# Sliding-window attention into a SwiGLU block: gather offsets in another order, batch 1's value products one place later, two more second-softmax transposes on the DMA crossbar

## The chip, the cores and the metric

The kernel runs on one core of a Trainium2 chip. The metric is the device time of one execution in microseconds (us); the time before is the median of three runs. Five engines work side by side, each through its own list of instructions in order: TensorE (PE), VectorE (DVE), ScalarE (ACT), GpSimd (POOL) and SyncE (SP). POOL and SP also issue DMA transfers, each on a queue of its own (q0 is POOL's, q1 is SP's), and sixteen DMA engines serve both queues.

## The reference

Attention over 8 batches of 8 heads, 576 positions and 64 dimensions, and behind it a gated feed-forward block over the 8 x 576 = 4608 tokens of 512 channels:

```python
mask = np.abs(pos[:, None] - pos[None, :]) <= 32
mask = mask | is_global[:, None] | is_global[None, :]      # 8 global positions
scores = np.where(mask, q @ k.T / sqrt(64), -1e9)
x = softmax(scores) @ v                                     # (b, h, s, d) -> (b*s, h*d)
g = x @ w_gate                                              # 512 -> 1536
out = (g * sigmoid(g) * (x @ w_val)) @ w_out                # 1536 -> 512
```

## The kernel before, in words

The feed-forward block is the backbone. The 4608 tokens are cut into nine chunks of 512, and a chunk is sixteen units: twelve `gate` units (one 128-wide slice of the hidden layer: four matmuls `pg`, four matmuls `pv`, then a tanh `th` on ACT and the products `gv` and `h` on DVE) and four `outp` units (twelve matmuls `po` each, a copy `osb` on ACT and a store). Between two units there is a gap with a number, and the attention of the next batch is dealt out over these gaps by a table written by hand: each batch's function `attention(b)` returns a dictionary from gap to steps. Batch 1's numbers count from gap 3, batch 2's from gap 16, batch 3's from gap 32, and so on by 16. Nothing reorders the steps afterwards: what stands in a gap stands there on every engine.

The steps of a batch, with the names of their tiles:

- `step_GT` turns the gathered and masked rows of the global keys and queries (`kqm`) on PE and copies them on DVE to `gT`.
- `step_S2` multiplies all keys `kT` by the global queries (the second softmax: global rows against all columns). ACT makes `p2e`, DVE multiplies it by the mask to `p`. `step_SG` multiplies all queries `qT` by the global keys in the same way (`pge`, `pg`). `step_S2` needs `kT` and `gT`, `step_SG` needs `qT` and `gT`.
- `step_P2T` turns `p` around into `p2t`. Below the batch number `XP` five PE transposes and one ACT copy do it; from `XP` on, one DMA transpose on SP's queue.
- `step_AV2` multiplies `p2t` by the values `va`; DVE makes `gvt` of it.
- `step_S(0..4)` are the score products of the window; ACT makes `pe`, DVE masks it to `pt`. `step_AV(0..3)` and `step_AV8` multiply these by `va`, by a copy of the values moved by 64 partitions (`vb`), and by `gvt`; DVE normalises to `xa`. `step_AV(tp)` needs the buffer `m` in PSUM that the one before it leaves when it is normalised.
- `step_X(tp)` turns `xa` into the block's input `xT`, from batch 2 on by DMA transposes on SP's queue.

From batch 2 on, keys and queries are first cast to bf16 in DRAM by POOL's queue (`kf`, `qf`) and then turned by two DMA transposes on SP's queue (`kT`, `qT`). Batch 0 runs ahead of the backbone in a head section, in which PE fills its waits with dummy matmuls `ps_w`. The head begins with small tables: a chain of short DVE instructions makes the row numbers `gofs` from which POOL's indirect DMAs gather the global rows `kg` and `qg`. POOL's loads of `va` and the weights stand behind these gathers. `va_clear` sets the borders of `va` by four memsets.

Of the kernel before, what the change touches and what calls it, by code (L numbers as in the profile page):

```python
# [9 lines left out]
FP32 = mybir.dt.float32  # L10
BF16 = mybir.dt.bfloat16
I32 = mybir.dt.int32
I64 = mybir.dt.int64
AF = mybir.ActivationFunctionType
ALU = mybir.AluOpType
AX = mybir.AxisListType

P = 128


def bc(ap, dims):

    return bass.AP(tensor=ap.tensor, offset=ap.offset, ap=[ap.ap[0]] + dims)
# [3 lines left out]
def kernel(  # L27
# [34 lines left out]
    const = ctx.enter_context(tc.tile_pool(name="const", bufs=1))  # L62
# [70 lines left out]
    gidx_i64 = const.tile([P, NG], I64)  # L133
# [6 lines left out]
    def load_0(name, hg):  # L140
# [13 lines left out]
    bofs_f = const.tile([P, 2, B // 2], FP32)  # L154
    nc.gpsimd.iota(bofs_f, pattern=[[0, 2], [2 * H * S, B // 2]], base=0, channel_multiplier=0,
                   allow_small_or_imprecise_dtypes=True)
# [40 lines left out]
    dmh = const.tile([P, 2, 2], FP32)  # L197
    nc.vector.tensor_tensor(out=dmh, in0=dmask[:, 0:2], in1=dmask[:, 2:4], op=ALU.add)
    mka = const.tile([P, 2, 2], FP32)
    nc.vector.tensor_reduce(  # L200
        out=mka, in_=oh16.rearrange("p h a r -> p a r h"), axis=AX.X, op=ALU.add
    )
    asel = const.tile([P, 2], FP32)
    nc.vector.tensor_reduce(out=asel, in_=mka, axis=AX.X, op=ALU.add)
    va_clear(0)
    hb = const.tile([P, 2], FP32)
    nc.vector.tensor_scalar(
        out=hb, in0=bc(asel[:, 1:2], [[-1, 2]]), scalar1=float(H * S), scalar2=None, op0=ALU.mult
    )
    nc.vector.tensor_tensor(  # L210
        out=bofs_f, in0=bofs_f, in1=bc(hb, [[1, 2], [0, B // 2]]), op=ALU.add
    )
# [6 lines left out]
    gidx_f = const.tile([P, NG], FP32)  # L219
    nc.vector.tensor_copy(  # L220
        out=gidx_f, in_=gidx_i64.bitcast(I32).rearrange("p (a b) -> p a b", b=2)[:, :, 0]
    )
    tmp8 = const.tile([P, NG], FP32)
    gcol = const.tile([P, 1], FP32)
    nc.vector.tensor_tensor(out=tmp8, in0=p8, in1=gidx_f, op=ALU.mult)
    nc.vector.tensor_reduce(out=gcol, in_=tmp8, axis=AX.X, op=ALU.add)
    ngcol = const.tile([P, 1], FP32)
    nc.vector.tensor_scalar(out=ngcol, in0=gcol, scalar1=-1.0, scalar2=None, op0=ALU.mult)
    nc.vector.tensor_scalar(
        out=hrow, in0=hrow, scalar1=float(S), scalar2=gcol, op0=ALU.mult, op1=ALU.add  # L230
    )
    nc.vector.tensor_scalar(out=gofs, in0=bofs_f, scalar1=hrow, scalar2=None, op0=ALU.add)
    R2 = (WIN + 0.5) ** 2
    thr = const.tile([P, 2], FP32)
    nc.vector.tensor_scalar(
        out=thr, in0=asel, scalar1=R2 + 0.25, scalar2=-0.25, op0=ALU.mult, op1=ALU.add
# [3 lines left out]
        out=sgn, in0=asel, scalar1=2.0, scalar2=-1.0, op0=ALU.mult, op1=ALU.add  # L240
# [2 lines left out]
    nc.vector.tensor_scalar(  # L243
        out=thi, in0=asel[:, 0:1], scalar1=1e6, scalar2=0.5, op0=ALU.mult, op1=ALU.add
    )

    def gather(i):
        kg = gw.tile([P, D], FP32, tag="kg", name="kg")
        qg = gw.tile([P, D], FP32, tag="qg", name="qg")
        for a, (dst, src) in enumerate(((kg, k), (qg, q))):  # L250
            nc.gpsimd.indirect_dma_start(
                out=dst, out_offset=None,
                in_=src.rearrange("b h s d -> (b h s) d"),
                in_offset=bass.IndirectOffsetOnAxis(ap=gofs[:, a, i : i + 1], axis=0),
            )
        return kg, qg
# [91 lines left out]
    def attention(b):  # L348
# [354 lines left out]
        L = lambda f, *a: (lambda: f(*a))  # L703
# [30 lines left out]
        if b == 1:  # L734
            return r | {
                5: [L(step_P2T), L(step_S, 0)],
                6: [L(step_S, 1), L(step_AV2)],
                7: [L(step_S, 2), L(step_AV, 0)],
                8: [L(step_S, 3), L(step_AV, 1)],
                9: [L(step_AV, 2)],  # L740
                10: [L(step_AV, 3), L(step_X01, 0)],
                11: [L(step_S, 4), L(step_X01, 1)],
                12: [L(step_AV8)], 13: [L(step_X8)],
            }
# [162 lines left out]
    for i, g in attention(1).items():  # L907
        gaps[3 + i] = gaps.get(3 + i, []) + g
# [56 lines left out]
```

## Time and profile before

| | |
|---|---|
| median of 3 runs | 357.86 us (357.67 to 358.93) |
| the profiled execution | 357.59 us |
| its span, first to last instruction | 355.7 us |
| PE busy | 348.3 us, 98% |
| DVE, ACT, POOL busy | 231.6, 151.9, 93.7 us |
| granted TensorE clock | 0.999 |

The profiled execution took 1.9 us more than its span, and 0.27 us less than the median. PE is nearly always at work, so a time on another engine or a queue counts only where PE waits for it.

### The profile page before, as it was taken

To read this page: it belongs to the slowest core of one execution; us is meant where nothing else is said; L and a number is where in the kernel's file an instruction comes from. 1 tells how busy PE (TensorE), PEld (TensorE's weight loads), DVE (VectorE), ACT (ScalarE), POOL (GpSimd) and SP (SyncE) were. 2 spreads that over 40 slices of the span, in tenths; PEclk is the share of its full clock that TensorE was granted. 3 is DMA by queue.
4 is the path that set the end of the run, shared out by engine and by line. 5 is a ranking of instruction groups with operands and counts; after the bars stand their busy time and mean duration, and the time that the engine had idled before them with its cause. 6 is when DMAs were issued, how large, how long until landed. Compare 5 with 4: busy or idle time off the path is not lost.

```text
span 355.7 us, 7729 instructions
## 1 busy us (share of the span) xinstructions
PE 348.3 (98%) x3161; PEld 168.0 (47%) x3161; DVE 231.6 (65%) x470; ACT 151.9 (43%) x235; POOL 93.7 (26%) x110
## 2 busy tenths in 40 slices
PE   7999999999999999999999999999999999999996
PEld 2574545444444454444444444444444444444444
DVE  5868784389818873789368935894488637815850
ACT  4865662465325541554244523543254323323322
POOL 8894663905325214301290111000000000000000
PEclk9999999999999999999999999999999999999999
DMA  7999999999999999995899979813330230011002
GB/s 104 156 196 204 184 211 161 166 252 141 157 166 233 140 155 153 180 180 80 147 164 157 138 120 168 115 40 92 101 73 2 61 100 28 0 59 62 0 20 101
DMA packets 153541, 44.15 MB, mean 124 GB/s; under 512 B 140065, under 2 KB 148001, under 8 KB 153505
## 3 DMA queue, kind: packets, MB, share of 16 engines
q0 software_dynamic: 101216, 19.14, 67.2%
q1 hardware_dynamic: 52288, 24.51, 33.2%
q8 instruction: 25, 0.41, 0.5%
q14 instruction: 12, 0.09, 0.1%
HBM read 38.02 MB, written 16.52 MB: 153 GB/s over the span
## 4 chain that ended last, share of the span: by engine, by line
PE 84%; DMA 9%; POOL 4%; DVE 1%; issue 1%; SPq 0%; ACT 0%; POOLq 0%
PE po L850 26%; PE pg L793 24%; PE pv L793 23%; DMA va<-in_v_dram 5%; PE ps_av L595 3%; PE ps_s L508 3%; DMA q_bf<-in_q_dram 3%; DMA vb<-va 2%; PE ps_av L586 1%; PE po L837 1%; POOL va L102 1%; PE ps_av L477 1%; PE ps_s L442 1%; PE ps_av L622 0%; PE ps_av L614 0%
## 5 line engine op out<-in xcount | busy, mean ns | idle before, releaser
L793 PE MATMUL pg<-xT,wg_sb 128*128 128x512 bf16 x420 | 108.1, 380 | 0.0
L793 PE MATMUL pv<-xT,wv_sb 128*128 128x512 bf16 x420 | 107.8, 379 | 0.0
L822 DVE SCALAR_TENSOR_TENSOR gv<-th,pg 128x512 bf16<-128x512 bf16 x107 | 73.3, 685 | 50.5 <-ACT th L820 49.5
L820 ACT ACTIVATE th<-pg 128x512 bf16<-128x512 f32 x107 | 63.9, 598 | 81.7 <-PE pg L793 81.2
L850 PE MATMUL po<-wo_sb,h 128*128 128x512 bf16 x420 | 94.6, 380 | 0.0
L826 DVE TENSOR_TENSOR h<-gv,pv 128x512 bf16<-128x512 bf16 x107 | 73.5, 687 | 11.5 <-PE pg L793 0.5
L793 PEld LDWEIGHTS <-wv_sb 128*128 128x128 bf16 x424 | 41.5, 98 | 50.0
L850 PEld LDWEIGHTS <-h 128*128 128x128 bf16 x420 | 39.5, 98 | 45.4
L793 PEld LDWEIGHTS <-wg_sb 128*128 128x128 bf16 x424 | 38.4, 98 | 43.5 <-issue 1.7
L102 POOL DMA_DIRECT2D va<-in_v_dram x40 | 35.0, 982 | 82.5 <-PE ps_av L595 77.7
L855 ACT ACTIVATE osb<-po 128x512 f32<-128x512 f32 x35 | 20.9, 597 | 81.9 <-PE po L850 79.9
L541 ACT ACTIVATE pe<-ps_s 128x1024 bf16<-128x1024 f32 (+1 forms) x39 | 36.4, 936 | 17.1 <-PE ps_s L508 17.1
L547 DVE TENSOR_TENSOR pt<-pe,band 128x1024 bf16<-128x1024 bf16 (+1 forms) x39 | 24.7, 634 | 14.0 <-ACT pe L541 14.0
L568 DVE TENSOR_TENSOR xa<-ps_av,den 128x512 bf16<-128x512 f32 (+1 forms) x40 | 25.5, 638 | 1.4
L562 DVE TENSOR_REDUCE den<-ps_av 128x8 f32<-128x16 f32 (+1 forms) x40 | 6.7, 167 | 27.6 <-PE ps_av L595 25.2
L508 PEld LDWEIGHTS <-kT 64*128 64x128 bf16 x576 | 10.7, 95 | 15.5 <-issue 15.1
L109 POOL DMA_DIRECT2D kf<-in_k_dram x6 | 13.4, 2240 | 15.9 <-issue 9.3
L109 POOL DMA_DIRECT2D qf<-in_q_dram x6 | 16.0, 2667 | 1.5 <-DMA qf<-in_q_dram 1.5
L508 PE MATMUL ps_s<-qT,kT 64*128 64x64 bf16 x576 | 15.3, 191 | 0.0
L595 PE MATMUL ps_av<-vb,pt 128*64 128x66 bf16 x256 | 14.2, 197 | 0.8 <-DMA vb<-va 0.8
L595 PE MATMUL ps_av<-va,pt 128*64 128x66 bf16 x256 | 14.4, 197 | 0.0
L595 PEld LDWEIGHTS <-pt 128*64 128x64 bf16 x512 | 10.8, 110 | 5.0 <-DMA vb<-va 0.9
(142 smaller groups left out, 200.3 us busy)
## 6 DMA issues: line engine op xcount, KB each, us to landing
out_dram<-osb SPq DMA_DIRECT2D x35, 256.0 KB, 2.3
vb<-va SPq DMA_DIRECT2D x14, 264.0 KB, 6.0
kf<-in_k_dram POOLq DMA_DIRECT2D x6, 576.0 KB, 16.4
qf<-in_q_dram POOLq DMA_DIRECT2D x6, 576.0 KB, 18.5
va<-in_v_dram POOLq DMA_DIRECT2D x24, 128.0 KB, 11.3
va<-in_v_dram POOLq DMA_DIRECT2D x16, 96.0 KB, 7.8
wg_sb<-in_moe_w_gate_dram POOLq DMA_DIRECT2D x3, 512.0 KB, 11.5
wv_sb<-in_moe_w_val_dram POOLq DMA_DIRECT2D x3, 512.0 KB, 13.3
```

The lines of the kernel that those rows point to most:

```text
L102: nc.gpsimd.dma_start(out=va[lo:hi, u, :, 0:D], in_=vs[t0 + lo : t0 + hi])
L109: nc.gpsimd.dma_start(out=t, in_=src[b].rearrange("h s d -> s h d"))
L508: nc.tensor.matmul(out=ps[:, par, 64 * slot : 64 * slot + 64], lhsT=kT[r : r + 64, hp, 64 * t : 64 * t + P], rhs=qTs[b][r : r + 64, hp, 64 ...
L541: nc.scalar.activation(out=pe, in_=ps[:, :, 0 : 64 * ns].rearrange("p r (s c) -> p r s c", c=64), func=AF.Exp, scale=SCALE,)
L547: mult = lambda: nc.vector.tensor_tensor(out=pt.rearrange("p r s c -> p (r s) c"), in0=pe.rearrange("p r s c -> p (r s) c"), in1=bc(band, ...
L568: nc.vector.tensor_tensor(out=xa.rearrange("p (g h) d -> p g h d", g=g), in0=bc(ps, pst + [[1, D]]), in1=bc(den, [[4, g], [1, 4], [0, D]]) ...
L595: nc.tensor.matmul(out=ps[64 * e : 64 * e + 64, hg, hl, :], lhsT=pt[:, hl % 2, 4 * (hl // 2) + 2 * (tp % 2) + e, :], rhs=(va if e == 0 els ...
L793: nc.tensor.matmul(out=ps[:, 0:n], lhsT=w[:, cc, P * fc : P * (fc + 1)], rhs=xT[:, cc, t0 : t0 + n], start=(cc == 0), stop=(cc == NCC - 1),)
L820: nc.scalar.activation(out=th[:, 0:n], in_=pg[:, 0:n], func=AF.Tanh, scale=0.5)
L822: nc.vector.scalar_tensor_tensor(out=gv[:, 0:n], in0=th[:, 0:n], scalar=1.0, in1=pg[:, 0:n], op0=ALU.add, op1=ALU.mult,)
L826: nc.vector.tensor_tensor(out=st["h"][:, fc, 0:n], in0=gv[:, 0:n], in1=pv[:, 0:n], op=ALU.mult)
L850: nc.tensor.matmul(out=po, lhsT=st["h"][:, fc, P * ts : P * (ts + 1)], rhs=wo_sb[:, fc, :], start=(fc == 0), stop=(fc == NFC - 1),)
```

## The change

There are three parts. First, the chain to `gofs`: the four memsets of `va_clear(0)` and the small table `dmh` go behind it, the base of the row numbers is now worked out from the table `i8_f` in place of a POOL iota of its own, the integer column is multiplied without a copy to float ahead of it, and everything is prepared up to the global column `gcol`, which comes in last. Second, batch 1's `step_AV(0)` and `step_AV(1)` go one gap later each. Third, `XP` is 2 in place of 4, so that batches 2 and 3 turn `p` by a DMA transpose on SP's queue too; in batch 2 `step_S2`, `step_SG` and `step_P2T` go to its gap 2 (they stood in gaps 3, 3 and 4), and `step_S(2)`, `step_AV(0)`, `step_S(3)`, `step_AV(1)` and their `step_X` go one gap earlier; in batch 3 `step_P2T` goes from gap 4 to gap 2.

```diff
-    XP = 4
+    XP = 2
...
-    va_clear(0)
-    hb = const.tile([P, 2], FP32)
-    nc.vector.tensor_scalar(
-        out=hb, in0=bc(asel[:, 1:2], [[-1, 2]]), scalar1=float(H * S), scalar2=None, op0=ALU.mult
-    )
-    nc.vector.tensor_tensor(
-        out=bofs_f, in0=bofs_f, in1=bc(hb, [[1, 2], [0, B // 2]]), op=ALU.add
-    )
...
+    hb = const.tile([P, 2], FP32)
+    nc.vector.tensor_scalar(
+        out=hb, in0=bc(asel[:, 1:2], [[-1, 2]]), scalar1=float(H), scalar2=hrow,
+        op0=ALU.mult, op1=ALU.add,
     )
+    bofs_f = const.tile([P, 2, B // 2], FP32)
+    nc.vector.scalar_tensor_tensor(
+        out=bofs_f, in0=bc(i8_f, [[0, 2], [1, B // 2]]), scalar=float(2 * H),
+        in1=bc(hb, [[1, 2], [0, B // 2]]), op0=ALU.mult, op1=ALU.add,
+    )
+    nc.vector.tensor_scalar(out=bofs_f, in0=bofs_f, scalar1=float(S), scalar2=None, op0=ALU.mult)
...
+    nc.vector.tensor_scalar(out=gofs, in0=bofs_f, scalar1=gcol, scalar2=None, op0=ALU.add)
...
+    va_clear(0)
...
-                7: [L(step_S, 2), L(step_AV, 0)],
-                8: [L(step_S, 3), L(step_AV, 1)],
-                9: [L(step_AV, 2)],
+                7: [L(step_S, 2)],
+                8: [L(step_S, 3), L(step_AV, 0)],
+                9: [L(step_AV, 1), L(step_AV, 2)],
...
-                3: [L(step_S2), L(step_SG)],
-                4: [L(step_S, 0), L(step_P2T)],
+                2: [L(step_S2), L(step_SG), L(step_P2T)],
+                4: [L(step_S, 0)],
                 6: [L(step_S, 1), L(step_AV2)],
-                8: [L(step_S, 2), L(step_AV, 0), L(step_X, 0)],
-                10: [L(step_S, 3), L(step_AV, 1), L(step_X, 1)],
+                7: [L(step_S, 2), L(step_AV, 0), L(step_X, 0)],
+                9: [L(step_S, 3), L(step_AV, 1), L(step_X, 1)],
```

On VectorE, in the head, the chain to `gofs` before (`hb` and `bofs_f` are the parts of the row number from batch parity and batch, `hrow` the head, `gcol` the global column):

```order
L180 MEMSET va_95 32x264
L181 MEMSET va_95 32x264
L207 TENSOR_SCALAR hb<-asel 128x2
L210 TENSOR_TENSOR bofs_f<-bofs_f,hb 128x8
L215 TENSOR_TENSOR tmp8h<-dmask,i_f 128x8
L218 TENSOR_REDUCE hrow<-tmp8h 128x1
L220 CAST gidx_f<-gidx_i_99 128x8
L225 TENSOR_TENSOR tmp_153<-p_129,gidx_f 128x8
L226 TENSOR_REDUCE gcol<-tmp_153 128x1
L228 TENSOR_SCALAR ngcol<-gcol 128x1
L229 TENSOR_SCALAR hrow<-hrow,gcol 128x1
L232 TENSOR_SCALAR gofs<-bofs_f,hrow 128x8
```

and the same place in the changed kernel:

```order
L203 TENSOR_TENSOR tmp8h<-dmask,i_f 128x8
L206 TENSOR_REDUCE hrow<-tmp8h 128x1
L208 TENSOR_SCALAR hb<-asel,hrow 128x2
L213 SCALAR_TENSOR_TENSOR bofs_f<-i_f,hb 128x8
L217 TENSOR_SCALAR bofs_f<-bofs_f 128x8
L220 TENSOR_TENSOR tmp_145<-p_127,gidx_i_99 128x8
L224 TENSOR_REDUCE gcol<-tmp_145 128x1
L225 TENSOR_SCALAR gofs<-bofs_f,gcol 128x8
L227 TENSOR_SCALAR ngcol<-gcol 128x1
L230 TENSOR_SCALAR thr<-asel 128x2
L234 TENSOR_SCALAR sgn<-asel 128x2
L238 TENSOR_SCALAR thi<-asel 128x1
```

The memsets now come behind `thi`, and `gofs` is the first instruction after `gcol`.

On ScalarE, in batch 2, before (each `th` is one gate; `p2e` and `pge` belong to `step_S2` and `step_SG`, `pe` to `step_S`):

```order
L820 ACTIVATE th<-pg 128x512 x3
L449 ACTIVATE p2e<-ps_s_1490 128x640
L427 ACTIVATE pge<-ps_sg 128x576
L820 ACTIVATE th<-pg 128x512
L541 ACTIVATE pe<-ps_s 128x1024
L471 COPY p2t<-ps_p2t 128x640
L820 ACTIVATE th<-pg 128x512 x2
L541 ACTIVATE pe<-ps_s 128x1024
L820 ACTIVATE th<-pg 128x512 x2
```

and in the changed kernel:

```order
L818 ACTIVATE th<-pg 128x512 x2
L447 ACTIVATE p2e<-ps_s_1467 128x640
L425 ACTIVATE pge<-ps_sg 128x576
L818 ACTIVATE th<-pg 128x512 x2
L539 ACTIVATE pe<-ps_s 128x1024
L818 ACTIVATE th<-pg 128x512 x2
L539 ACTIVATE pe<-ps_s 128x1024
L818 ACTIVATE th<-pg 128x512
```

`step_S2` and `step_SG` have moved ahead of one gate, the copy of `p2t` is gone, and the third score product follows its predecessor after one gate.

On SyncE, the queue around batch 2, before (`vb` is batch 2's, the `kT` and `qT` below it are batch 3's, `xT<-xa` is batch 2's output):

```order
L857 DMA out_dram<-osb 128x512 x4
L129 DMA vb<-va_95 64x2112
L130 DMA vb<-va_95 64x2112
L116 DMA_TRANSPOSE kT_98<-kf_1428 128x4x576
L120 DMA_TRANSPOSE qT<-qf_1430 128x4x576
L633 DMA_TRANSPOSE xT<-xa 128x4x128 x3
```

and in the changed kernel:

```order
L855 DMA out_dram<-osb 128x512 x4
L129 DMA vb<-va_95 64x2112
L130 DMA vb<-va_95 64x2112
L461 DMA_TRANSPOSE p2t<-p_1478 128x5x128
L116 DMA_TRANSPOSE kT_98<-kf_1425 128x4x576
L120 DMA_TRANSPOSE qT<-qf_1427 128x4x576
L631 DMA_TRANSPOSE xT<-xa 128x4x128 x3
```

The transpose of `p` stands between the copies `vb` and the next batch's key transpose; batch 3's stands at the same place one batch on.

More of the change, by code (lines that the diff above doesn't have):

```diff
@@ L153 @@
                    allow_small_or_imprecise_dtypes=True)
-    bofs_f = const.tile([P, 2, B // 2], FP32)
-    nc.gpsimd.iota(bofs_f, pattern=[[0, 2], [2 * H * S, B // 2]], base=0, channel_multiplier=0,
-                   allow_small_or_imprecise_dtypes=True)
     iq = const.tile([P, KC], FP32)
@@ L196 @@
     nc.vector.tensor_tensor(out=dmask, in0=oh16[:, :, 0, :], in1=oh16[:, :, 1, :], op=ALU.add)
-    dmh = const.tile([P, 2, 2], FP32)
-    nc.vector.tensor_tensor(out=dmh, in0=dmask[:, 0:2], in1=dmask[:, 2:4], op=ALU.add)
     mka = const.tile([P, 2, 2], FP32)
@@ L218 @@
     nc.vector.tensor_reduce(out=hrow, in_=tmp8h, axis=AX.X, op=ALU.add)
-    gidx_f = const.tile([P, NG], FP32)
-    nc.vector.tensor_copy(
-        out=gidx_f, in_=gidx_i64.bitcast(I32).rearrange("p (a b) -> p a b", b=2)[:, :, 0]
-    )
+    hb = const.tile([P, 2], FP32)
+    nc.vector.tensor_scalar(
+        out=hb, in0=bc(asel[:, 1:2], [[-1, 2]]), scalar1=float(H), scalar2=hrow,
+        op0=ALU.mult, op1=ALU.add,
+    )
+    bofs_f = const.tile([P, 2, B // 2], FP32)
[4 more added lines that the diff above has]
+    nc.vector.tensor_scalar(out=bofs_f, in0=bofs_f, scalar1=float(S), scalar2=None, op0=ALU.mult)
     tmp8 = const.tile([P, NG], FP32)
     gcol = const.tile([P, 1], FP32)
-    nc.vector.tensor_tensor(out=tmp8, in0=p8, in1=gidx_f, op=ALU.mult)
+    nc.vector.tensor_tensor(
+        out=tmp8, in0=p8, in1=gidx_i64.bitcast(I32).rearrange("p (a b) -> p a b", b=2)[:, :, 0],
+        op=ALU.mult,
+    )
     nc.vector.tensor_reduce(out=gcol, in_=tmp8, axis=AX.X, op=ALU.add)
+    nc.vector.tensor_scalar(out=gofs, in0=bofs_f, scalar1=gcol, scalar2=None, op0=ALU.add)
     ngcol = const.tile([P, 1], FP32)
     nc.vector.tensor_scalar(out=ngcol, in0=gcol, scalar1=-1.0, scalar2=None, op0=ALU.mult)
[L229 to L232, printed above, removed]
     R2 = (WIN + 0.5) ** 2
@@ L245 @@
     )
+    va_clear(0)
+    dmh = const.tile([P, 2, 2], FP32)
+    nc.vector.tensor_tensor(out=dmh, in0=dmask[:, 0:2], in1=dmask[:, 2:4], op=ALU.add)
     def gather(i):
```

## The prediction

> **What bounds the kernel now.** I read the page first: engine shares, and the chain that ended last.
>
> ```profile
> PE 348.3 (98%) x3161; PEld 168.0 (47%) x3161; DVE 231.6 (65%) x470; ACT 151.9 (43%) x235; POOL 93.7 (26%) x110
> PE 84%; DMA 9%; POOL 4%; DVE 1%; issue 1%; SPq 0%; ACT 0%; POOLq 0%
> ```
>
> PE is busy 348.3 of 355.7 us. So an edit can only take instructions off PE, or one of PE's waits, or add a wait. The wait of PE that the change aims at (us in total, times, longest):
>
> ```profile
> PE ps_av L595 <- DMA vb<-va: 0.8, 1, 0.8
> ```
>
> Only the wait for the first instruction at the start is longer. This one is batch 1's `vb`; next comes one on DVE in batch 2. Their places, in PE's order of time (start, duration, in brackets the idle time before it):
>
> ```profile
> 48.84 0.22 PE L595 MATMUL ps_av<-va,pt 128*64 128x66 bf16 x1
> 49.82 0.22 PE L595 MATMUL ps_av<-vb,pt 128*64 128x66 bf16 x1 [0.76 <-DMA vb<-va]
> 92.44 0.28 PE L586 MATMUL ps_av<-gvt,pg 64*128 64x264 bf16 x2 [0.38 <-DVE xa L568]
> ```
>
> Products with `va` and `vb` are issued in pairs, so batch 1's wait costs 49.82 - 48.84 = 0.98 us. That and 0.38 us are all the waiting that the moved value products can save.
>
> **The head.** Rows of DVE, POOL and PE:
>
> ```profile
> 5.37 0.23 DVE L232 TENSOR_SCALAR gofs<-bofs_f,hrow 128x8 int32<-128x8 f32 x1
> 4.64 0.68 POOL L142 DMA_DIRECT2D q_bf<-in_q_dram  x1
> 5.88 1.05 POOL L251 DMA_INDIRECT kg<-in_k_dram,gofs  x1 [0.57 <-DVE thi L243]
> 9.26 0.76 DVE L371 COPY qT<-ps_t 128x576 bf16<-128x576 bf16 x1 [1.79 <-PE ps_t L365]
> 12.00 0.29 DVE L261 TENSOR_TENSOR kqm<-kg,mka 128x128 bf16<-128x128 f32 x1 [0.38 <-DMA kg<-in_k_dram,gofs]
> 12.49 0.39 PE L344 MATMUL ps_w<-ident 128*128 128x512 bf16 x1
> 12.72 0.27 PE L403 MATMUL ps_g<-ident,kqm 128*128 128x128 bf16 x2
> 13.03 0.29 DVE L409 COPY gT<-ps_g 128x256 bf16<-128x256 bf16 x1
> ```
>
> POOL waits 0.57 us for `gofs`; its issue of `q_bf` ends at 5.32. One iota less on POOL and an earlier `gofs` let the gather start some 0.5 us sooner, and not more, since POOL itself is busy to there. DVE's wait for `kg` (0.38) may go. But PE's turn of `kqm` at 12.72 follows a dummy matmul without idle time, and DVE's copy `gT` at 13.03 follows that turn: PE's dummies set the pace, so the head ends when it ended. I count **0**. The earlier issue also moves POOL's loads, but the DMA engines are busy from the second slice on (tenths, 40 slices of 8.9 us):
>
> ```profile
> DMA  7999999999999999995899979813330230011002
> ```
>
> So the casts that later steps wait for come 0 to 0.5 us sooner; I take 0.2 where it matters. The memsets behind `gofs` are covered by DVE's 1.79 us of idle time before 9.26; without that cover they would cost about 1 us.
>
> **Batch 1.** `step_AV(0)` starts one gate later, after `vb` has landed. All its instructions are the same, and the next three value products find their buffers free: an `outp` of twelve matmuls now lies between `step_AV(0)` and `step_AV(1)`. PE arrives at chunk 1 **0.98 us earlier**.
>
> **Batch 2, the part that decides.** PE before (one gate is `pg` and `pv`):
>
> ```profile
> 71.95 1.03 PE L793 MATMUL pg<-xT,wg_sb 128*128 128x512 bf16 x4
> ...
> 73.77 0.46 PE L442 MATMUL ps_s<-kT,gT 128*32 128x320 bf16 x8
> 74.06 0.42 PE L420 MATMUL ps_sg<-qT,gT 128*32 128x288 bf16 x8
> ...
> 76.58 0.45 PE L467 MATMUL ps_p2t<-ident,p 128*128 128x128 bf16 x5
> 76.87 1.03 PE L793 MATMUL pg<-xT,wg_sb 128*128 128x512 bf16 x4
> ...
> 80.75 0.47 PE L477 MATMUL ps_av<-va,p2t 128*32 128x132 bf16 x20
> ```
>
> The transposes cost PE 76.87 - 76.58 = **0.29 us**, once in batch 2 and once in batch 3. ACT's copy of `p2t` (0.69) hides beside the gates anyway.
>
> But `step_S2` and `step_SG` go one gate earlier, to 71.95, and PE comes 0.98 sooner: `step_SG` would start at 71.95 + 0.29 - 0.98 = 71.26. It needs batch 2's `qT`. SP's row, and the DMA view's median time from issue to landing for that transfer:
>
> ```profile
> 62.50 5.16 SPq L120 DMA_TRANSPOSE qT<-qf  x1
> qT<-qf SPq DMA_TRANSPOSE x1, 10.1
> ```
>
> `qT` lands at 62.50 + 10.1 = 72.6. It stood 1.46 us ahead of `step_SG`; now PE waits 1.34 us for it. The 0.98 us of batch 1 are gone and 0.36 us more, less what the head gives (0.2). After the 0.29 us saved, `step_AV2` comes at 80.75 + 0.36 - 0.29 = 80.82, with the head's 0.2 at 80.6: about where it was.
>
> Next, `p2t` must be there by 80.6. DVE made `p` 1.76 us after `step_S2` began:
>
> ```profile
> 75.04 0.49 DVE L454 TENSOR_TENSOR p<-p2e,mg 128x640 bf16<-128x640 bf16 x1
> 70.57 0.55 SPq L130 DMA_DIRECT2D vb<-va  x1
> vb<-va SPq DMA_DIRECT2D x2, 264.0 KB, 8.7
> 79.46 5.62 SPq L116 DMA_TRANSPOSE kT<-kf  x1
> ```
>
> So `p` is ready at 71.95 - 0.98 + 1.76 = 72.73; SP has been free since 71.12 and takes it at once. How long it flies there, no run shows: later batches took 2.6 to 7.7 us, batch 4's being the nearest, since casts fill POOL's queue and `vb` (issued at 146.07) is ahead of it there as well:
>
> ```profile
> DMA to landing us min/median/max: 2.6/6.0/7.7
> 149.12 2.05 SPq L463 DMA_TRANSPOSE p2t<-p  x1
> p2t<-p SPq DMA_TRANSPOSE x1, 7.7
> q1 hardware_dynamic: 417, 0.11, 80.2%
> q0 software_dynamic: 415, 0.05, 79.4%
> ```
>
> By 7.7 it lands at 80.45: just in time, **0**. The bounds are 75.3 (by 2.6) and what the second rival gives. The last two rows are one microsecond (115 to 116 us) with both queues full: 417 and 415 packets, so SP's queue gets half there. The Trainium skill (VectorE: DVE Perf Modes, The three transpose paths and Rules for kernel authors) advises TensorE for a 128x128 transpose if the result may go to PSUM, with 390 ns against 1309 ns for the crossbar, a rule against this change. The estimate from that page for five tiles is 6.5 us, a landing at 79.2, by which the sum would stay; the trace's 2.6 and 7.7 lie on both sides.
>
> Queued behind the new transpose on SP are batch 3's `kT` and `qT`. `kT` waited for its cast until 79.46 anyway, and the transpose takes about 2 us of SP's time, so the issue order costs nothing. In flight it takes packets from the casts, so `kT`, `qT` and `xT` behind them may slip by up to 1 us. Batch 2's `xT` has a deadline:
>
> ```profile
> 92.73 4.16 SPq L633 DMA_TRANSPOSE xT<-xa  x3
> xT<-xa SPq DMA_TRANSPOSE x2, 7.7
> 104.59 1.03 PE L793 MATMUL pg<-xT,wg_sb 128*128 128x512 bf16 x4
> ```
>
> The third issue is at about 95.5 and lands at 103.2; chunk 2 reads it at 104.59. So PE can be at most 1.4 us ahead there, 0.4 if it slips by 1. In the forecast it is ahead by 0.13 from `step_AV2` and by 0.38 from the `xa` wait, because `step_AV(1)` now has two gates to be normalised in: 0.5, which fits or nearly so.
>
> **Batch 3** saves its 0.29. Its order on PE is otherwise the same:
>
> ```profile
> 111.24 0.48 DVE L454 TENSOR_TENSOR p<-p2e,mg 128x640 bf16<-128x640 bf16 x1
> 120.41 0.47 PE L477 MATMUL ps_av<-va,p2t 128*32 128x132 bf16 x20
> ```
>
> `p` to `step_AV2` is 120.41 - 0.29 - 111.72 = 8.4 us, over the longest 7.7: no wait. `kT` and `qT` of batch 4 are issued up to 7 us later on SP; batch 4's `step_S2` is eleven units away from batch 3's `step_AV2`, so that costs 0.
>
> **The sum.** 0.98 (batch 1) - 1.34 (`qT`) + 0.2 (head) + 0.29 + 0.38 + 0.29 = 0.8 us; I take off 0.2 for a part of the `xT` or `p2t` margins being used up: **0.6 us faster**. The profiled execution took 357.59 (its span and 1.9), so 357.0; the median is 0.27 above it: **357.26**.
>
> **Rivals.**
>
> *All waits go and nothing new is late.* `qT` would have to land 1.3 us sooner, or the head pull the whole stream forward. For it: the chain that ended last runs through POOL's first loads and batch 1's `vb`. Against it: the queue is full, and 0.5 us is all that POOL gains. Gain 0.98 + 0.38 + 0.58 = 1.94, held by the `xT` deadline to about 1.7: **356.2**. Chance 0.16.
>
> *The new transpose lies behind `vb` (slower).* Place: batch 2's `step_AV2`. `vb` lands at 70.57 + 8.7 = 79.27. In batch 4 `p2t` landed 3.1 us after its `vb` (149.12 + 7.7 against 146.07 + 7.6, rows below). If that distance holds, `p2t` comes at 82.4, and PE waits 1.8 us: 0.6 - 1.8, so 1.2 slower, **359.1**. With 4 us behind `vb` it would be 360.0. It decides from a landing at 81.2 on; over 0.5% slower needs 83.0. Against it: the trace has packets of SP's queue in 73 to 77 us and few after 78, so `vb` has nearly left by then.
>
> ```profile
> 146.07 0.48 SPq L130 DMA_DIRECT2D vb<-va  x1
> vb<-va SPq DMA_DIRECT2D x1, 264.0 KB, 7.6
> q1 hardware_dynamic: 5, 0.01, 3.8%
> ```
>
> (The last row is 78 to 79 us.) The Trainium skill (DMA: Bandwidth & Descriptors, Queues, rings and completion order) says that an SDMA engine consumes one queue's descriptors in ring order and takes turns between queues by packets; the 417 to 415 above agree, and by that rule this rival's order is certain, only the distance is open. Chance 0.2.
>
> *The moves do nothing measurable*: `qT` later still by the added traffic, or the value products of batch 2 held by DVE one gate after `step_AV2`. Gain 0 to 0.2: **357.7**. Chance 0.1, the forecast has 0.54.
>
> **How the numbers follow.** A measurement of this kernel can tell about 0.5%, 1.8 us, from no change. The forecast (357.26, own range 356.5 to 358.0) and the third rival lie within. Of the first rival's 0.16 some 0.12 lies below 356.07; of the second's 0.2 some 0.09 lies above 359.65. Faster 0.12, same 0.79, slower 0.09. The range leaves out a little of both ends: 356.1 to 359.3.
>
> **What would show it.** Right: no idle time before batch 1's product with `vb`; PE's longest new wait is `step_SG` on `qT`, about 1.1 to 1.3 us; `step_AV2` of batch 2 within 0.5 us of 80.75; chunk 2 starts 0.3 to 0.6 us earlier than 104.59; no ACT copy `p2t` in batches 2 and 3. Wrong: no wait on `qT` (then the first rival, chunk 2 over 1 us earlier), or a wait of `step_AV2` on `p2t` of over 0.6 us (the second), or a wait of chunk 2's first gate on `xT`.

## The result, and the profile after

The changed kernel took 358.11 us (median of 4 runs, 357.24 to 358.62), the kernel before 357.76 (4 runs, 357.61 to 358.93): ratio 1.0, 95% interval 0.9971 to 1.0029. A second set, run later beside e5 to e7, gave 359.79 us (10 runs, 357.44 to 362.64) against 357.93 (31 runs): ratio 1.0061, interval 1.0035 to 1.0087. In six of those ten runs the mean granted clock (the share of its full speed that TensorE was given) was 0.990 to 0.995 instead of 1.0; they took 359.58 to 362.64 us, the other four 357.44 to 358.78. Both sets count: no difference that can be told in the first, a loss of 0.6% in the second. Runs e6 and e7 below show a wait behind which the clock drops; none of the changed kernel's own low-clock runs has a profile.

The profiled execution of the first set took 358.0 us (span 356.2) against 357.59 (span 355.7). From its page, engine shares and the chain that ended last:

```profile
PE 344.0 (97%) x3102; PEld 167.0 (47%) x3151; DVE 231.9 (65%) x469; ACT 150.8 (42%) x233; POOL 92.5 (26%) x109
PE 76%; DMA 16%; POOL 5%; issue 1%; DVE 1%; ACT 0%; POOLq 0%
```

PE's busy time fell by 4.3 us and the span did not: DMA's part of the chain went from 9% to 16%. (Not all of the 4.3 us is time off PE: of the 59 records fewer, ten are the transposes, worth 0.58 us; matmul records can be missing from a trace.) PE's waits behind the head (us in total, times, longest):

```profile
PE ps_sg L418 <- DMA qT<-qf: 0.9, 1, 0.9
...
PE ps_av L593 <- DMA vb<-va: 0.6, 1, 0.6
PE ps_av L475 <- DMA p2t<-p: 0.4, 1, 0.4
```

Of these three, only the one on `vb` was there before (0.8). PE's rows at those places, and at the two where batch 2 and batch 3 hand on (line numbers are two lower than before):

```profile
50.34 0.22 PE L593 MATMUL ps_av<-va,pt 128*64 128x66 bf16 x1
...
51.18 0.22 PE L593 MATMUL ps_av<-vb,pt 128*64 128x66 bf16 x1 [0.62 <-DMA vb<-va]
...
71.35 0.46 PE L440 MATMUL ps_s<-kT,gT 128*32 128x320 bf16 x8
72.70 0.43 PE L418 MATMUL ps_sg<-qT,gT 128*32 128x288 bf16 x8 [0.90 <-DMA qT<-qf]
...
81.35 0.47 PE L475 MATMUL ps_av<-va,p2t 128*32 128x132 bf16 x20 [0.43 <-DMA p2t<-p]
...
104.69 1.04 PE L791 MATMUL pg<-xT,wg_sb 128*128 128x512 bf16 x4
...
120.41 0.47 PE L475 MATMUL ps_av<-va,p2t 128*32 128x132 bf16 x20
```

`step_AV2` of batch 2 starts at 81.35 (before 80.75), chunk 2 at 104.69 (104.59), `step_AV2` of batch 3 at 120.41 (120.41). SP's rows, and the DMA view's time from issue to landing, say why:

```profile
62.72 5.18 SPq L120 DMA_TRANSPOSE qT<-qf  x1
...
70.82 0.55 SPq L130 DMA_DIRECT2D vb<-va  x1
73.13 1.64 SPq L461 DMA_TRANSPOSE p2t<-p  x1
...
111.87 1.21 SPq L461 DMA_TRANSPOSE p2t<-p  x1
```

```profile
qT<-qf SPq DMA_TRANSPOSE x1, 9.9
p2t<-p SPq DMA_TRANSPOSE x1, 8.2
p2t<-p SPq DMA_TRANSPOSE x1, 8.5
```

62.72 + 9.9 = 72.6 is where `step_SG` starts, 73.13 + 8.2 = 81.3 where batch 2's `step_AV2` does, 111.87 + 8.5 = 120.4 where batch 3's does. At each of these places PE starts when a transfer lands. (The third wait is too short to stand in its row: PE took 120.41 - 104.69 = 15.72 us from chunk 2 to there, against 15.54 in e8, where `p2t` landed ahead of it. So it is about 0.2 us.)

### The profile page after: what moved, and what is told of

Read it like the earlier page. It is cut to its first block, busy times and chain, and to the rows that moved or that the text cites. A ratio compares the mean times of both kernels' runs of the same rounds, so it can differ in the third digit from the quotient of the medians.

```text
span 356.2 us, 7657 instructions
## 1 busy us (share of the span) xinstructions
PE 344.0 (97%) x3102; PEld 167.0 (47%) x3151; DVE 231.9 (65%) x469; ACT 150.8 (42%) x233; POOL 92.5 (26%) x109
## 4 chain that ended last, share of the span: by engine, by line
PE 76%; DMA 16%; POOL 5%; issue 1%; DVE 1%; ACT 0%; POOLq 0%
PE po L848 25%; PE pg L791 21%; PE pv L791 20%; DMA p2t<-p 5%; DMA k_bf<-in_k_dram 3%; DMA va<-in_v_dram 3%; PE ps_av L593 3%; DMA qT<-qf 3%; PE ps_s L506 2%; DMA vb<-va 2%; POOL va L102 1%; PE ps_av L584 1%; PE po L835 1%; PE ps_av L475 1%; PE ps_s L440 1%
## 5 line engine op out<-in xcount | busy, mean ns | idle before, releaser
L791 PE MATMUL pg<-xT,wg_sb 128*128 128x512 bf16 x400 | 106.9, 380 | 1.7 <-issue 0.2
L791 PE MATMUL pv<-xT,wv_sb 128*128 128x512 bf16 x413 | 106.6, 379 | 0.1
L848 PE MATMUL po<-wo_sb,h 128*128 128x512 bf16 x399 | 92.4, 379 | 0.9 <-issue 0.2
L593 PEld LDWEIGHTS <-pt 128*64 128x64 bf16 x512 | 10.8, 110 | 4.9 <-DMA vb<-va 0.7
```

What stands on the lines that cost most here:

```text
L593: nc.tensor.matmul(out=ps[64 * e : 64 * e + 64, hg, hl, :], lhsT=pt[:, hl % 2, 4 * (hl // 2) + 2 * (tp % 2) + e, :], rhs=(va if e == 0 els ...
L791: nc.tensor.matmul(out=ps[:, 0:n], lhsT=w[:, cc, P * fc : P * (fc + 1)], rhs=xT[:, cc, t0 : t0 + n], start=(cc == 0), stop=(cc == NCC - 1),)
L848: nc.tensor.matmul(out=po, lhsT=st["h"][:, fc, P * ts : P * (ts + 1)], rhs=wo_sb[:, fc, :], start=(fc == 0), stop=(fc == NFC - 1),)
```

## The experiments

Theory A: where PE waits for a single transfer, time saved ahead of that place becomes wait. Its rivals stand with the runs. Each run has its ratio to the kernel before, measured in the same set, with its 95% interval; the ratio differs by up to 0.13% from the quotient of the two medians. There are three sets, each on a chip of its own: e1 to e4, e5 to e8, and e9 to e12.

**e1: the head alone.** The changed kernel with the old tables for batches 1 and 2 and the old limit:

```diff
-    XP = 2
+    XP = 4
-                7: [L(step_S, 2)],
-                8: [L(step_S, 3), L(step_AV, 0)],
-                9: [L(step_AV, 1), L(step_AV, 2)],
+                7: [L(step_S, 2), L(step_AV, 0)],
+                8: [L(step_S, 3), L(step_AV, 1)],
+                9: [L(step_AV, 2)],
...
```

> Only the first part: the chain to gofs in the new order, all else as before. Theory A (PE is held to the arrival of single transfers, and time saved ahead of such a place is given back there): PE is some 0.4 us earlier at chunk 0 and waits for batch 1's vb longer by as much, 1.2 to 1.4 us in place of 0.98; the product with vb comes at 49.8 to 51.2 us, and the time is that of before within 0.3 us. Rival B (the head's gain lasts): the product with vb and all behind it come 0.4 us earlier, time 0.4 us less.

Measured: 357.47 us, ratio 0.9978 (0.9952 to 1.0005): no difference that can be told. Over all profiles of this study PE's first batch-1 turn (`ps_g`) came at 35.10 to 36.06 us in the eleven with the new head and at 35.63 to 35.96 in the three with the old one, 0.2 us sooner in the mean and within the scatter. In this profile PE lost time in batch 1 at another place:

```profile
49.59 0.28 PE L584 MATMUL ps_av<-gvt,pg 64*128 64x264 bf16 x2 [1.12 <-DVE gvt L490]
```

DVE and ACT both sat idle until 48.8 us there; the trace does not show for what, and I leave it open. It cost less than it looks, since the product with `vb` came at 50.07 us and PE's load of weights had still to wait 0.2 us for `vb` there. That place lies within the 49.8 to 51.2 us of theory A.

**e2: batch 1's value products alone**, in the kernel before.

```diff
-                7: [L(step_S, 2), L(step_AV, 0)],
-                8: [L(step_S, 3), L(step_AV, 1)],
-                9: [L(step_AV, 2)],
+                7: [L(step_S, 2)],
+                8: [L(step_S, 3), L(step_AV, 0)],
+                9: [L(step_AV, 1), L(step_AV, 2)],
```

> Only the second part: batch 1's step_AV(0) and step_AV(1) one gap later. Theory A: the wait for vb is 0 to 0.6 us in place of 0.98, by when vb lands (49.8 in the run before, 51.2 in the changed one); batch 2's step_SG has 1.46 us to spare and doesn't wait; what is saved, 0.4 to 0.98 us, reaches chunk 2 and the end, since batch 2's xT lands at about 103.2 and chunk 2 begins at 103.7 to 104.2. Rival B (the move alone is worth its wait): 0.98 us less, no wait for vb at all.

Measured: 357.85 us, ratio 0.9987 (0.9954 to 1.0019). PE's rows of batch 1:

```profile
51.08 0.22 PE L595 MATMUL ps_av<-va,pt 128*64 128x66 bf16 x1
51.09 0.22 PE L595 MATMUL ps_av<-vb,pt 128*64 128x66 bf16 x1
```

The pair follows without the 0.98 us between them. PE starts chunk 1 at 65.74 (before 66.54), batch 2's `step_AV2` at 79.96 (80.75) and the last products at 349.12 (349.89): 0.8 us that stays to the end of this profile. The time did not move by an amount that ten runs can tell.

**e3: the second softmax of batch 2 early and by the crossbar (and of batch 3)**, without the head and without batch 1's move.

```diff
-    XP = 4
+    XP = 2
-                3: [L(step_S2), L(step_SG)],
-                4: [L(step_S, 0), L(step_P2T)],
+                2: [L(step_S2), L(step_SG), L(step_P2T)],
+                4: [L(step_S, 0)],
...
```

> Only the third part: DMA transposes of p in batches 2 and 3 with batch 2's new table. Theory A: step_SG waits 0.3 to 0.5 us for qT (72.6 against 72.24), step_AV2 of batch 2 waits 0.9 to 1.4 us for p2t (issue at about 73.8, flight 8.2 us, landing at 82.0) and comes at 81.7 to 82.2 against 80.75 before; the wait on xa (0.38) is gone; batch 3's step_AV2 waits 0.1 to 0.3 us: in all 0.5 to 1.0 us slower. Rival B (the two transposes are worth what they take off PE): 0.58 + 0.38 us less the 0.36 us wait, 0.6 us faster.

Measured: 359.11 us, ratio 1.0029 (1.0006 to 1.0053): slower. The waits are there though PE comes 0.9 us later than in the changed kernel, the one on `qT` longer and the one on `p2t` shorter than expected (two of its rows):

```profile
73.43 0.43 PE L420 MATMUL ps_sg<-qT,gT 128*32 128x288 bf16 x8 [0.74 <-DMA qT<-qf]
...
81.97 0.47 PE L477 MATMUL ps_av<-va,p2t 128*32 128x132 bf16 x20 [0.31 <-DMA p2t<-p]
```

So the third part of the change is a loss by itself. It is not a gain that batch 1's move spoils. Whether the early gate (`step_S2` and `step_SG` in batch 2's gap 2) or the crossbar (the transpose by DMA) makes the loss, this run does not tell; e12 shows the part of the gate.

**e4 and e10: the change without the early gate and the crossbar.** Batch 2's transposes stay on PE, `step_S2` and `step_SG` stay at their old gate; the head, batch 1's move and the earlier value products of batch 2 are kept.

```diff
-    XP = 2
+    XP = 4
-                2: [L(step_S2), L(step_SG), L(step_P2T)],
-                4: [L(step_S, 0)],
+                3: [L(step_S2), L(step_SG)],
+                4: [L(step_S, 0), L(step_P2T)],
```

> The changed kernel without its DMA transposes: XP = 4 again, batch 2's step_S2 and step_SG in gap 3 and step_P2T in gap 4 on PE as before; head, batch 1 and the earlier step_AV of batch 2 as changed. Theory A: the wait for vb is 0 to 0.9 us, no wait of step_SG and step_AV2, no wait on xa; chunk 2 begins 0.8 to 1.3 us earlier than in the run before (103.3 to 103.8 us), held by xT at 103.2 to 103.4, and so does the end: 0.7 to 1.2 us faster than before and 0.8 to 1.5 us faster than the changed kernel. Rival B: without the 0.58 us saved on PE it is slower than the changed kernel by as much.

> The version that took least so far, once more: batch 2's softmax transposed on PE and step_S2 and step_SG one gate later than in the changed kernel, the rest as changed. Theory A: no wait of PE over 0.4 us behind the head, the last products start at 348.5 to 349.2 us, no run below a clock of 0.998, time 0.4 to 1.3 us below the kernel before. Rival G (its gain in the first set was chance): ratio 0.999 to 1.002.

Measured: 357.27 us, ratio 0.9974 (0.995 to 0.9999), and again 357.07 us, ratio 0.9969 (0.9949 to 0.9989): faster by 0.3% in both sets, with a clock of at least 0.999 in all 22 runs. The first profile (356.19 us) has chunk 2 with no wait, at 103.25; the second, of a longer run (357.91 us), has the next bound, and not the absence of waits that I expected:

```profile
103.25 1.02 PE L791 MATMUL pg<-xT,wg_sb 128*128 128x512 bf16 x4
```

```profile
104.98 1.02 PE L791 MATMUL pg<-xT,wg_sb 128*128 128x512 bf16 x4 [1.01 <-DMA xT<-xa]
```

`xT` of batch 2 lands in time in the first profile and a microsecond late in the second. That caps what can be had ahead of chunk 2.

**e5: `vb` behind the new transpose in SP's queue.**

```diff
-                1: [L(step_GT), vb],
-                2: [L(step_S2), L(step_SG), L(step_P2T)],
+                1: [L(step_GT)],
+                2: [L(step_S2), L(step_SG), L(step_P2T), vb],
```

> The changed kernel with batch 2's load of vb issued behind step_P2T instead of ahead of it. Theory A (PE is held to the arrival of single transfers, and the new p2t lies behind vb in SP's queue): p2t, issued at 73.1 us as before, now lands by 79.5 us instead of 81.3; step_AV2 of batch 2 has no wait (0.4 us in the changed kernel) and starts at about 80.9 us instead of 81.35. vb, issued at about 74.8 instead of 70.3, lands at about 83 us and step_AV(0), which comes at about 83.5, waits 0 to 0.5 us for it. Time 0 to 0.4 us below the changed kernel. Rival B (the transpose takes its 8 us in flight because of the casts, whatever stands ahead of it in its own queue): p2t lands at 81.3 again, the wait of 0.4 us stays, and vb comes late as well.

Measured: 358.01 us, ratio 1.0005 (0.999 to 1.0019). SP's rows, the time to landing, and PE's rows of this kernel:

```profile
72.85 1.26 SPq L461 DMA_TRANSPOSE p2t<-p  x1
74.29 0.47 SPq L129 DMA_DIRECT2D vb<-va  x1
```

```profile
p2t<-p SPq DMA_TRANSPOSE x1, 6.7
```

```profile
73.16 0.43 PE L418 MATMUL ps_sg<-qT,gT 128*32 128x288 bf16 x8 [1.64 <-DMA qT<-qf]
...
81.32 0.47 PE L475 MATMUL ps_av<-va,p2t 128*32 128x132 bf16 x20
```

`p2t` lands at 72.85 + 6.7 = 79.55, and `step_AV2` does not wait. With `vb` ahead the same flight took 7.9 to 9.5 us in six profiles. So by this one profile the place behind `vb` costs it 1.2 to 2.8 us; the other 6.7 us are not `vb`'s. PE gained nothing at `step_AV2`, because `qT` came later in this run and held PE first. The time is nevertheless below that of the changed kernel in the same set (ratio 1.0061, e8), because none of the ten runs has a low clock. Why, no run shows: `qT` flew 10.4 us here and 10.8 to 11.4 in the other three profiles of the set, so its wait may be the shorter one in most runs.

**e7: `step_SG` one gate later, the transpose left where it is.**

```diff
-                2: [L(step_S2), L(step_SG), L(step_P2T)],
+                2: [L(step_S2), L(step_P2T)],
+                3: [L(step_SG)],
```

> The changed kernel with step_SG of batch 2 one gate later (behind step_S2 and step_P2T instead of between them). The wait of 0.9 us on qT goes, since qT lands at 72.6 us and step_SG comes at about 73.5. Theory A (the arrivals set the time, not the waits): step_AV2 comes 0.9 us sooner and waits for p2t until 81.2 to 81.4 us, so its wait grows from 0.4 to 1.2 to 1.4 us; chunk 2 at 104.5 to 104.7 us, time within 0.2 us of the changed kernel. Rival D (each wait is a loss of its own): step_AV2 of batch 2 at about 80.5, chunk 2 at about 103.8 and the time 0.9 us below the changed kernel.

Measured: 358.66 us, ratio 1.0033 (1.0013 to 1.0053). The wait on `qT` is gone, and the one on `p2t` is in its place, larger than expected since the flight took 9.1 us. PE's rows, with the gate that follows:

```profile
82.29 0.73 PE L475 MATMUL ps_av<-va,p2t 128*32 128x132 bf16 x20 [2.20 <-DMA p2t<-p]
82.96 1.89 PE L792 MATMUL pg<-xT,wg_sb 128*128 128x512 bf16 x4
84.64 1.59 PE L792 MATMUL pv<-xT,wv_sb 128*128 128x512 bf16 x4
```

Rival D falls: the wait moved to the next arrival. (The median lies 1.1 us below that of e8, about as rival D had it, but by the number of low-clock runs, four here and six there; the runs at a clock of 0.999 or 1.0 have medians of 358.6 here and 358.3 there.) But these rows show something that neither theory had. The halves of a gate take 1.02 to 1.04 us in the other profiles' rows above. The stage view (length of the stretch, busy time of PE and four other units, then granted clock, DMA share and GB/s):

```profile
82.00:82.50 0.50, 0.21 (x12) 0.21 (x16) 0.00 (x0) 0.00 (x0) 0.50 (x1) 0.85 2.48 159
...
83.00:85.00 2.00, 2.00 (x9) 0.69 (x6) 0.68 (x3) 0.12 (x1) 0.87 (x1) 0.50 2.43 155
...
85.50:86.00 0.50, 0.50 (x3) 0.14 (x1) 0.49 (x1) 0.00 (x0) 0.50 (x1) 0.74 2.34 159
86.00:86.50 0.50, 0.50 (x20) 0.32 (x18) 0.40 (x2) 0.00 (x0) 0.50 (x1) 1.00 1.61 159
```

Behind the idle 2.20 us the granted clock is 0.50. From 0.85 in the first row and 0.74 in the third the stretch runs from 82.35 to 85.76, 3.41 us. From `step_AV2` to `step_AV(0)` PE needs 86.40 - 82.29 = 4.11 us here, 83.83 - 81.35 = 2.48 in the changed kernel's first profile: the wait cost 1.63 us more than its length.

**e6: no `p2t` to wait for.** `step_AV2` of batches 2 and 3 multiplies with the constant table `mg2`; the transposes are issued and not read.

```diff
-                        lhsT=st["p2t"][:, u, 32 * hp : 32 * hp + 32],
+                        lhsT=(mg2.rearrange("p (u c) -> p u c", c=P) if b in (2, 3) else st["p2t"])[:, u, 32 * hp : 32 * hp + 32],
```

> The changed kernel, but step_AV2 of batches 2 and 3 multiplies with a constant table (mg2) in the place of p2t; the transposes by DMA are still issued, nobody reads them. Theory A: step_AV2 of batch 2 starts at about 80.9 us (no wait), that of batch 3 at 119.7 to 119.9 us instead of 120.41, the last products of PE at 349.2 to 349.5 us instead of 349.96: time 0.5 to 0.7 us below the changed kernel. Rival C (the next arrival, that of xT for chunk 2, gives it back): chunk 2 starts at 104.6 to 104.7 us as before and the last products at 349.9; PE then waits for xT ahead of chunk 2, or at step_AV(0) of batch 3.

Measured: 359.62 us, ratio 1.0034 (1.0012 to 1.0057); five of ten runs at a clock of 0.994 to 0.995 and 359.92 to 360.63 us. The question it was built for stays open, since the profile fell on such a run:

```profile
73.78 0.43 PE L418 MATMUL ps_sg<-qT,gT 128*32 128x288 bf16 x8 [2.27 <-DMA qT<-qf]
...
75.31 1.91 PE L791 MATMUL pv<-xT,wv_sb 128*128 128x512 bf16 x4
```

It answered another, with the stage view of the same stretch:

```profile
74.50:75.00 0.50, 0.50 (x3) 0.21 (x2) 0.05 (x1) 0.41 (x1) 0.00 (x0) 0.71 1.25 317
...
75.50:77.50 2.00, 2.00 (x7) 0.66 (x5) 0.93 (x2) 0.60 (x1) 0.00 (x0) 0.50 1.24 343
...
78.00:78.50 0.50, 0.50 (x4) 0.18 (x3) 0.00 (x0) 0.00 (x0) 0.00 (x0) 0.88 1.19 218
```

From 0.71 and 0.88 the stretch at half clock runs from 74.71 to 78.12, 3.41 us again. So a wait on `qT` alone can be followed by it, without any wait on `p2t`.

**e8: the changed kernel again**, in one set with e5 to e7.

> The changed kernel itself, as the measure for the three others of this set: PE waits 0.4 to 1.0 us for qT in batch 2 and 0.2 to 0.8 us for p2t, the last products start at 349.6 to 350.3 us; the ratio to the kernel before within 0.998 to 1.003.

Measured: 359.79 us, ratio 1.0061 (1.0035 to 1.0087), outside what I expected, by the six low-clock runs. Its profile fell on the fastest of the ten (357.44 us): a wait of 0.99 us on `qT`, none above 0.2 on `p2t`, last products at 349.36.

```profile
72.75 0.43 PE L418 MATMUL ps_sg<-qT,gT 128*32 128x288 bf16 x8 [0.99 <-DMA qT<-qf]
...
80.99 0.47 PE L475 MATMUL ps_av<-va,p2t 128*32 128x132 bf16 x20
...
104.27 1.03 PE L791 MATMUL pg<-xT,wg_sb 128*128 128x512 bf16 x4
```

This is the run that the prediction describes: chunk 2 comes 0.32 us and the last products 0.53 us earlier than in the profile before. The same kernel took up to 5 us more in other runs of the set.

**e9: the wait on `qT` filled.** Four dummy matmuls ahead of `step_SG`.

```diff
-                2: [L(step_S2), L(step_SG), L(step_P2T)],
+                2: [L(step_S2), L(warm, 512, 512, 512, 512), L(step_SG), L(step_P2T)],
```

> The changed kernel with four dummy matmuls of 512 columns (0.86 us of PE, results unused) between step_S2 and step_SG of batch 2, where PE waits for qT. Theory E (a PE wait of about 2 us or more halves the granted clock for some 3.4 us, and that is what makes the changed kernel's slower runs): the dummies leave 0.1 to 1.4 us of that wait, so the clock of nearly all runs is 0.998 to 1.0 (6 of 10 were at 0.995 or less without them), all runs lie at 357.2 to 359.0 us, and the median is 1.0 to 1.8 us below that of the changed kernel in the set before, at 0.998 to 1.003 of the kernel before. Rival F (the clock drops for another reason, or p2t's wait is what drops it): as many runs at 0.995 as without the dummies, and a median of 359 to 360 us.

Measured: 358.58 us (357.72 to 359.47, 12 runs), ratio 1.0013 (1.0 to 1.0026). PE's rows (the profiled run took 359.34 us):

```profile
72.03 1.04 PE L342 MATMUL ps_w<-ident 128*128 128x512 bf16 x4
73.33 0.43 PE L418 MATMUL ps_sg<-qT,gT 128*32 128x288 bf16 x8 [0.27 <-DMA qT<-qf]
```

The clock was 0.998 to 1.0 in all twelve runs, as theory E has it. Three of them lie above the 359.0 us that it gave; the profiled one, which is one of the three, has two waits on `p2t`, 0.45 us in batch 2 and 0.56 in batch 3. Without the dummies `step_SG` would have waited 73.33 - 71.64 - 0.29 = 1.4 us in this profile.

Theory E is supported, not shown. The changed kernel's 1.0061 is from another set, on another chip, and was not measured beside e9. In the set of e9, e12 has the same early gate without dummies and had two low-clock runs of twelve, too few to tell from none. And the first set of the changed kernel, 1.0 without dummies, had none in four.

**e11: batch 3 by the crossbar, batch 2 on PE.** The kernel of e10 with another limit:

```diff
-    XP = 4
+    XP = 3
```

> The version with batch 2 on PE, but batch 3's transposes by DMA as in the change: 0.29 us less on PE. Theory A: p2t of batch 3, issued at about 110.6 us, lands 8.2 to 8.5 us later, at 118.8 to 119.1, and step_AV2 of batch 3 would come at 118.8: the wait is 0 to 0.3 us, and the time within 0.3 us of the version with PE in both. Rival (the 0.29 us are kept): step_AV2 of batch 3 at 118.8 without a wait, the last products 0.29 us sooner.

Measured: 357.97 us, ratio 0.9979 (0.9951 to 1.0006), against 0.9969 for e10 beside it: the 0.29 us cannot be seen in the time. PE's rows:

```profile
104.59 1.02 PE L791 MATMUL pg<-xT,wg_sb 128*128 128x512 bf16 x4 [0.90 <-DMA xT<-xa]
...
120.13 0.47 PE L475 MATMUL ps_av<-va,p2t 128*32 128x132 bf16 x20
```

From chunk 2 to batch 3's `step_AV2` PE takes 15.54 us, against 15.82 in e10: up to here the saving is kept, as the rival has it. Batch 4's `step_AV2`, at 157.56, then waits 0.27 us for its own `p2t`, and the last products come 245.38 us after chunk 2, against 245.31 in e10. So theory A holds one batch later than I expected.

**e12: the wait on `qT` alone.** The kernel of e10 with `step_S2` and `step_SG` one gate earlier.

```diff
-                3: [L(step_S2), L(step_SG)],
+                2: [L(step_S2), L(step_SG)],
```

> The version with batch 2 on PE, but step_S2 and step_SG of batch 2 one gate earlier, as in the change: the wait on qT alone, with no transpose by DMA. Theory A and E: step_SG comes at 71.3 and waits 1.2 to 2.3 us for qT, step_AV2 of batch 2 comes 1.2 to 2.3 us later than in the version without (79.9), at 81.1 to 82.2, and stays that late to the end: 1.2 to 1.5 us over that version in most runs, and some 3 us over it in those whose wait passes 2 us (clock 0.995). Rival H (the wait on qT is given back further on, since p2t and xT set the time): step_AV(0) to chunk 2 at 103.3 us as in the version without, the same time.

Measured: 358.87 us, ratio 1.0013 (0.9988 to 1.0039), against 0.9969 (0.9949 to 0.9989) for e10. PE's row, and the flight of `qT` in the DMA view:

```profile
74.37 0.43 PE L418 MATMUL ps_sg<-qT,gT 128*32 128x288 bf16 x8 [2.89 <-DMA qT<-qf]
```

```profile
qT<-qf SPq DMA_TRANSPOSE x1, 11.7
```

Chunk 2 starts at 106.15 (103.25 and 104.98 in the two profiles without the early gate) and the last products at 351.76 (348.57 and 350.29). Rival H falls: the early gate costs 1.5 to 3.2 us of PE's time by these profiles, 1.8 us by the medians of one set. The wait was longer than expected. By theory E the clock should have dropped behind it, and it did not (0.999 over this run; the stage view right behind the wait):

```profile
74.00:76.00 2.00, 1.63 (x14) 0.72 (x15) 0.46 (x1) 0.85 (x2) 0.00 (x0) 1.00 1.21 318
76.00:78.00 2.00, 2.00 (x11) 0.88 (x9) 1.37 (x2) 0.87 (x2) 0.00 (x0) 1.00 1.24 342
```

It did drop in two of the twelve runs (360.40 and 360.61 us, both at 0.995).

## Why the prediction was right, and where not

The time was forecast as within 0.5% of the kernel before, 357.26 us in a range from 356.1 to 359.3. The first set (358.11, ratio 1.0) is within it and 0.85 us above the forecast; the second (359.79) lies beyond its upper end. The gain of 0.6 us was not found in either.

The main step was right: `step_SG` at the early gate waits for `qT`, and the wait takes what batch 1's move saves (e12 against e10, 1.8 us). Two steps were not: `p2t` was put down as no wait, and a wait of PE was priced at its length alone. That the four runs of the first set all had a clock of 0.998 or 0.999 was luck as far as the prediction goes, since nothing in it told them from the six of the second set.

Of the signs that it named, the two profiles of the changed kernel (the first set's and e8) have the longest new wait on `qT` in both, 0.90 and 0.99 us in place of 1.1 to 1.3; `step_AV2` of batch 2 0.60 and 0.24 us behind 80.75, where 0.5 was allowed; and chunk 2 0.10 us later and 0.32 us earlier. Idle time before batch 1's product with `vb` is in the first alone. No sign of being wrong is in either.

- **Head, 0 on PE and 0.2 on the casts.** The gather started 0.4 us sooner in all eleven profiles with the new head (5.49 or 5.50, against 5.88 or 5.89 in the three others). PE began chunk 0 at 21.27 us in their mean, against 21.34: 0 is right within the scatter. Batch 2's `qT` was issued 0.4 us sooner in the mean (62.36 against 62.79) but landed no sooner (73.3 against 73.0, in the ten and three profiles that have its landing), so nothing shows the 0.2.
- **Batch 1, 0.98 us.** Right: PE came to chunk 1 at 65.75 us in the mean of the ten other profiles with the move, against 66.75 in the three without, and none of the ten waits for `vb`. In the changed kernel's first profile the term failed: `vb` landed at 51.13 (43.03 + 8.10, from the chain that ended last), the product with it started at 51.18 (49.82 before), and the pair waited 51.18 - 50.34 = 0.84 us. I took one landing time for a constant.
- **`qT`, 1.34 us.** The wait is where the prediction put it: 0.90 and 0.99 us in the changed kernel, 0.74 in e3, 1.64 in e5, 2.27 in e6, 2.89 in e12, a mean of 1.6. The term was mis-sized in its spread: one flight of 10.1 us stood for 9.9 to 11.7.
- **Transposes off PE, 0.29 us each.** Taken off. In the first profile batch 2's and batch 3's `step_AV2` start when `p2t` lands, so they are not seen in the time; in e8 batch 3's does not wait and keeps it.
- **`p2t`, flight 7.7 us and no wait: the step that failed.** Flights with `vb` ahead were 7.9 to 9.5 us in batch 2, so waits were 0 to 0.45 us behind a wait on `qT`, and 2.20 us in e7 without one. This is the second rival's mechanism: in all six profiles with `vb` ahead, `p2t` lands 1.7 to 2.1 us behind the second `vb` (in the first one at 81.31, and `vb` at 70.82 + 8.7 = 79.52), however long it flies itself, and with `vb` behind it (e5) it flies 6.7 us. It came out cheaper than the rival's 1.8 us, because the distance was not the 3.1 us of batch 4 and PE was ready at 80.92 in place of 80.6. The Trainium skill (DMA: Bandwidth & Descriptors, Queues, rings and completion order) says that a DMA engine takes the descriptors of one queue in ring order; these landings agree with it. The Trainium skill (VectorE: DVE Perf Modes, The three transpose paths and Rules for kernel authors) advises TensorE for a 128x128 transpose whose result may go to PSUM, which is against the move. The kernels with both transposes on PE (e4, e10) are the faster ones, but their gate is the old one too, and e11 shows no difference for batch 3's alone, so no run here separates it. All flights of batches 2 and 3, 6.7 to 9.5 us, lay above the estimate of 6.5 us from that page.
- **`xT` as the next deadline, 1.4 us ahead at most.** The place is right, the size is not fixed: e4 starts chunk 2 at 103.25 without a wait, e10 and e11 wait 1.01 and 0.90 us there, until 104.98 and 104.59. The changed kernel never got so far ahead.
- **`xa`, 0.38 us.** The wait is gone in all profiles with the earlier value products (e4, for one, has no wait there). e1 and e2 keep it, 0.39 and 0.38 us. In its place a wait of 0.2 to 0.4 us on `xa` appeared in batch 1 in four of the profiles (e4, e9, e10, e12), where two value products now share a gate.
- **Batch 3, no wait.** 8.5 us of flight against 8.4 available: `step_AV2` at 120.41 to the hundredth as before. Of its 0.29 us, 0.1 went as PE came later to chunk 2 and about 0.2 as a wait.
- **What no step had: the granted clock.** I priced a wait of PE at its length. In e7 and e6 a wait of 2.2 us was followed by 3.41 us at half clock, worth 1.6 us; low-clock runs of the changed kernel take about 2 us more than its others (medians 360.4 and 358.3 us). In the set of e5 to e8, on one chip, the kernel before had none of 31 runs at 0.995 or less, the changed one six of ten. Over all sets, the kernels that wait for `qT` at the early gate (the changed one, e3, e5, e6, e12) had 14 of 56, e7 with its wait on `p2t` 4 of 10, those with the old gate (e4, e10, e11) and e9 none of 46. e1 and e2 had one in ten each, the kernel before 6 of 97 in the three later sets; what these waited for is not in a profile. So that such a wait lowers the clock is seen in two profiles; that it is behind every low-clock run is not shown.

Two slips in the prediction weigh nothing: 72.73 + 7.7 is 80.43, not 80.45, and the wait next in length after batch 1's is one of 0.44 us on `k_bf` in the head, just ahead of the 0.38 us on `xa`.

What stays open: why a wait of 2.20 or 2.27 us lowered the clock and one of 2.89 us did not; whether filling the wait keeps the clock up; what batch 2's crossbar transpose would cost with `step_S2` and `step_SG` at the old gate, which no run has; e1's idle time on DVE and ACT; and what e6 was built for, how much of the wait on `p2t` would reach the end of the kernel.

## What to carry to other kernels

Where an engine waits for a transfer, read the landing time in several executions before an instruction is moved up against it: here one place varied by 1.8 us, more than every saving of the change. A step that is moved up past a transfer's landing gives back what was saved ahead of it, so move first what the transfer depends on. Where a transfer lies behind another in the same queue, count from the landing of that one and not from its own issue: here `p2t`'s flight varied by 1.6 us, its distance behind `vb` by 0.4. And a wait on TensorE can have two prices, its length and a stretch at half clock behind it, which came after two of four waits of 1.6 to 2.9 us in these profiles. Dummy matmuls in the wait may take the second away (e9); that is not shown.

## What the runs showed of the hardware that I had not expected

- After a TensorE wait of 2.20 us (e7) and of 2.27 us (e6) the granted clock was 0.50 for 3.41 us; after one of 1.64 us (e5) and one of 2.89 us (e12) it stayed at 1.00. So the length alone does not decide. In both cases the whole wait lies within the 3.41 us ahead of the drop (e7: 80.09 to 82.29, the drop at 82.35; e6: 71.51 to 73.78, the drop at 74.71). The Trainium skill (TensorE: Matmul & The Clock Gate, Part 1) tells of a free-running window of about 3.4 us, and the length of the half-clock stretch agrees with it. The Trainium skill (TensorE: Matmul & The Clock Gate, Why this matters for your kernels) advises no idle gaps over about 3 us between matmul bursts; that bound does not hold here, 2.2 us was enough. That the place of the wait in such a window decides would fit all four waits; no run here shows it.
- The same transpose by DMA (`qT` of batch 2, same place in its queue) took 9.9 to 11.7 us to land from one kernel's profile to the next, 9.9 and 10.8 in the two of the changed kernel. `p2t` took 7.9 to 9.5 us with `vb` ahead of it, and landed 1.7 to 2.1 us behind `vb` each time.
